# A written order for the middle stage of an attention and two-MLP kernel

## The chip, the cores and the metric

The kernel runs on one core of a Trainium2 chip. The metric is the device time of one execution in microseconds (us). A core has five engines with a queue each, and every queue is worked in order: PE (TensorE, matmuls; its weight loads are shown as PEld), DVE (VectorE), ACT (ScalarE), POOL (GpSimd) and SP (SyncE, which here issues nearly all DMAs). An instruction waits at the head of its queue until what it needs is done; what stands behind it waits too.

## The reference, cut to what matters

Linear attention over 8 batches, 8 heads, 576 positions and 64 channels, then two MLPs over 4608 tokens of width 512 with a hidden width of 2048, all in float32:

```python
q_s = exp(q - max(q, -1));  q_s /= sum(q_s, -1) + 1e-9
k_s = exp(k - max(k, 2));   k_s /= sum(k_s, 2) + 1e-9        # over the positions
kv = einsum('bhsd,bhse->bhde', k_s, v);  x = einsum('bhsd,bhde->bhse', q_s, kv)
h = x @ w_in;   x = (h * clip(h + 3, 0, 6) / 6) @ w_out       # first MLP
h = x @ w2_in;  out = (h * sigmoid(h)) @ w2_out               # second MLP
```

## The kernel before, in words

The 4608 tokens are nine blocks of 512. A block has four attention units, one for each pair of heads; unit u belongs to block u // 4, so there are 36 units. Float32 matmuls of the MLPs are made of three passes over operands that were split into a high and a low part (high x high, high x low, low x high), each 128x512; a split costs one copy on ACT (high) and one subtraction on DVE (low).

The program has three stages, and no barrier stands between them:

- `first_block()` (L852) computes units 0 to 7 and part of 8, splits the first MLP's weights, and runs the first MLP on block 0. `spin` (L873) adds matmuls without use to keep PE occupied at the start.
- `middle()` (L1017) computes the other units, runs the first MLP on blocks 1 to 6, splits and sums the weights for the second MLP and writes them to DRAM (`Parts`, `Resident`, `Split`), and prepares the first operands of the next stage (`first_operands`, L1265). Its main step (j, f) is `mm1` (L552, twelve 128x512 matmuls into a PSUM bank "h", in four chunks c), the gate of four jobs (`Gate`, L564: relu on ACT, times_h on DVE, upper on ACT, lower on DVE), and `mm2` (L621, twelve matmuls into y0 to y3: eight that need the gate's upper part alone, four that need the lower part). A unit's small PE jobs lie between these: `k_turn`, `k_spread`, `kv_mm`, `q_turn`, `x_mm`.
- `second_mlp()` (L1335) runs the rest by events in order of a clock of PE slots. Its first PE work is the product P1 with operand B11 (high and low), then P6 with T2, then the last `mm2` of the middle's steps (L1671), then P5 (T1), P2 (B21), P7 (T3), P3 (B22).

What sets the order in the first two stages is a planner, `Plan`. `add` (L748) notes a job: its engine, an assumed duration, a key, the jobs that it needs, and the buffers that it takes and gives back. `once` (L753) then plays the jobs through in Python while the program is built: whenever an engine is free, the ready job with the lowest key starts, if its buffers are free. The order in which jobs started is the order in which the instructions are written, and so that of each queue. `plan.run(0, 300e3)` (L1187) does this once for `middle`, with keys from the tables `LATE`, `WORK` and `FETCH`. Waits between engines come from data and buffers, whatever the order.

Buffers that matter here: "t2k" (five 128x512 temporaries), "sp" (three), "h" and "a" (two PSUM banks each), and the 128x128 tiles `kvt` of which there are `KVS` = 5, one for each unit's kv, used in turn. `k_max` (L360) puts its half-way maximum m2 into a t2k buffer. `kv_mm(u)` waits for `x_mm(u - 1)` in the planner, since its kv takes the place of an older one that `x_mm(u - 1)` reads last.

The operands of P1 to P7 come from four blocks of the first MLP's output (B12, B22, B11, B21, loaded by SP) by four sums on POOL (t3, t1, t2, t4, L1239) and seven splits: high parts on ACT (L1300), low parts on DVE (L1310). t2 is in place over t3's result and needs the split T3 done and t1; t4 is in place over t2's result and needs the split T2 done; T4 needs t4. B11 needs only that t2 and t1 have read it. In the order before, T1, T2, B11, T4, B21 and B22 follow each other over the last 55 us of the stage, and the B22 split is the only one that is left when the last `mm2` of the stage runs.

Of the kernel before, what the change touches and what calls it, by code (L numbers as in the profile page):

```python
# [28 lines left out]
def efficient_attention_then_two_mlps(  # L29
# [20 lines left out]
    KCH = S // P  # L50
    TAIL = S - KCH * P
    NU = B * NP
    KVS = NP + 1
    NCL = NB - 2
    FAR = 4
    LAG = (2, 3)
# [15 lines left out]
    ident = const.tile([P, P], F32, name="ident")  # L72
    minus = att.tile([P, DM], F32R, tag="sp", bufs=3, name="minus")[:, 0:P]
    peaks = const.tile([P, P], F32, name="peaks")
    kvt = [const.tile([P, P], F32, name=f"kv{i}") for i in range(KVS)]
    vbufs = const.tile([P, 2, KCH + 1, 2, D + 1], F32, name="vbuf")
    small = const.tile([P, 8], F32, name="small")
# [280 lines left out]


    def k_max(u):  # L360
        t = kbuf[u]
        m1 = peaks.rearrange("p (h d) -> p h d", h=2)
        m2 = tmp.tile([P, 8, D], F32, tag="t2k", name="m2")[:, 0:4]
        m2 = m2.rearrange("p (h a) d -> p h a d", h=2)
        nc.vector.tensor_tensor(out=m2, in0=t[:, :, 0:2, :], in1=t[:, :, 2:4, :], op=ALU.max)
        nc.vector.tensor_tensor(out=m1, in0=m2[:, :, 0, :], in1=m2[:, :, 1, :], op=ALU.max)
        nc.vector.tensor_tensor(out=m1, in0=m1, in1=t[:, :, KCH, :], op=ALU.max)
        live["m1", u] = m1
# [370 lines left out]
    class Plan:  # L739
# [277 lines left out]
    def middle():  # L1017
# [12 lines left out]
        def unit(u):  # L1030
            j, pr = divmod(u, NP)
            key = lambda r: begin[u] + r + 0.3
            old, has_k = u == NP * 2, u < NU
            if u > NP * 2 + 2:
                n_q[u] = dma(0.8, key(-3.4), lambda: load_q(u), 256, [qsub[u - 2]])
            if has_k and u > NP * 2 + 1:
                n_k[u] = dma(0.7, key(-3.5), lambda: load_k(u), 320, [ksub.get(u - 2)])
                n_v[u] = dma(1.0, key(-2.5), lambda: load_v(u), 320, [kvmm[u - 2]])
            kx = qn = None
            if not old:  # L1040
                qm = add("DVE", 0.7, key(0), lambda: q_max(u), [n_q.get(u)])
                qs = add("POOL", 1.1, key(1), lambda: q_sub(u, nc.gpsimd), [qm], ["qe"], [], True)
                qsub[u] = qs
                qx = add("ACT", 0.65, key(2), lambda: q_exp(u), [qs])
                qa = add("DVE", 0.7, key(2), lambda: q_sum(u), [qx])
                qa = add("POOL", 0.3, key(2), lambda: q_eps(u, nc.gpsimd), [qa])
                qa = add("DVE", 0.22, key(2), lambda: q_recip(u), [qa])
                qn = add("POOL", 1.1, key(2), lambda: q_norm(u, nc.gpsimd), [qa], [], [], True)
            else:
                qsub[u] = None  # L1050
            if has_k and not old:
                km = add(
                    "DVE", 1.1, key(0), lambda: k_max(u), [n_k.get(u)], ["m1", "t2k"], ["t2k"], True
                )
                kt = add("PE", 0.12, key(1), lambda: k_turn(u, a_pool), [km], ["a", "mx"], ["m1"])
                kd = add("DVE", 0.3, key(1), lambda: k_peak(u), [kt], [], ["a"])
                ks = add("PE", 0.12, key(2), lambda: k_spread(u, a_pool), [kd], ["a", "ke"], ["mx"])
                kx = ksub[u] = add("DVE", 0.85, key(2), lambda: k_sub(u), [ks], [], ["a"])
            if u < DIRECT:
                qt_ = add("PE", 0.65, key(3), lambda: q_turn(u), [qn], ["a"], ["qe"])  # L1060
                ql = add("ACT", 0.62, key(3), lambda: q_copy(u), [qt_], ["qT"], ["a"])
            else:
                qb = add("DVE", 0.72, key(3), lambda: q_blocks(u), [qn], ["t2k"], ["qe"])
                z0 = dma(0.35, key(3), lambda: q_store(u), 256, [qb], [], ["t2k"])
                ql = dma(1.4, key(4), lambda: q_load(u), 256, [z0], ["qT", "z"])
            if has_k:
                kx = add("ACT", 0.78, key(3), lambda: k_exp(u), [kx])
                mm = kvmm[u] = add(
                    "PE", 0.48, key(4), lambda: kv_mm(u, a_pool),
                    [kx, n_v.get(u), xmm.get(u - 1)], ["a"], ["ke"],  # L1070
                )
                va = add("DVE", 0.45, key(4), lambda: kv_sum(u), [mm])
                vlow[u] = add("ACT", 0.55, key(4), lambda: kv_scale(u), [va], [], ["a"])
            xm = xmm[u] = add(
                "PE", 1.0, key(6), lambda: x_mm(u), [ql, vlow.get(u), vlow.get(u - NP)], ["a"],
                ["qT"] if u < DIRECT else ["qT", "z"],
            )
            first = ["x"] if pr == 0 and j < NCL else []
            if j < FAR:
                xu = add(  # L1080
                    "ACT", 0.62, key(6), lambda: x_upper(u), [xm, xready.get((j, 0))], first
                )
                xready[j, pr] = add("DVE", 0.69, key(6), lambda: x_lower(u), [xu], [], ["a"])
                return
            xc = add("ACT", 0.62, key(6), lambda: x_upper(u), [xm], ["t2k"], ["a"])
            xs_ = dma(0.35, key(6), lambda: x_store(u), 256, [xc], [], ["t2k"])
            if j < NCL:
                at = j * NF - 14 + 2 * pr + FETCH[(j - FAR) * NP + pr]
                ld = dma(
                    0.35, at, lambda: load_x(j, pr), 256, [xs_, xready.get((j, 0))], ["t2k"] + first  # L1090
                )
                hi = add("ACT", 0.64, at + 1.5, lambda: x_high(j, pr), [ld])
                xready[j, pr] = add("DVE", 0.72, at + 1.5, lambda: x_low(j, pr), [hi], [], ["t2k"], True)
# [49 lines left out]
        for n, s in list(enumerate(steps))[NF - 1 : NCL * NF]:  # L1143
            ph, j, f = s
            g3 = g2 = None
            if n >= NF:
                m = None
                for c in range(NC):
                    m = add(
                        "PE", 0.69, n - 0.5, lambda s=s, c=c: mm1(s, [c]), [xready.get((j, c)), m],  # L1150
                        ["h"] if c == 0 else [],
                        (["x"] if f == NF - 1 and c == NC - 1 else [])
                        + (["wi"] if j == NCL - 1 and c == NC - 1 else []),
                    )
                free[n] = m
                g = Gate(s)
                g0 = add("ACT", 0.62, n - 0.45, g.relu, [m], ["r"])
                g1 = add("DVE", 0.7, n - 0.45, g.times_h, [g0], [], ["r"])
                g2 = add("ACT", 0.62, n - 0.45, g.upper, [g1], ["g"])
                g3 = add("DVE", 0.7, n - 0.45, g.lower, [g2], [], ["h"])  # L1160
                plan.held |= {g0, g1, g2, g3}
# [22 lines left out]
            else:  # L1184
                pair_at[at] = add(eng, us, base + key, fn, deps, take, [], port)

        for fn in plan.run(0, 300e3):  # L1187
            fn()

    pair_at = {}  # L1190
# [74 lines left out]
    def first_operands():  # L1265
# [11 lines left out]
        def load(name):  # L1277
            def do():
                operand(name, 1)
                x_steps(1)[name.lower()]()  # L1280
            return do
# [4 lines left out]
            ("r1", "SP", 0.35, 1.5, get(1), 512, ("r0",), ["wi"], False),  # L1286
        ]
        for n, name in enumerate(("B22", "B11", "B21")):
            jobs.append((name.lower(), "SP", 0.35, 2.5 + n, load(name), 512, ("r1",), ["wi"], False))

        def total(name, key, deps):
            jobs.append((name, "POOL", 2.1, key, lambda: x_steps(1)[name](), 0, deps, [], True))
# [455 lines left out]
```

## Time and profile before

| | us |
|---|---|
| median of three runs (1572.47 to 1573.20) | 1572.76 |
| the profiled execution | 1573.41 |
| its span, first to last instruction | 1571.70 |
| PE busy in the span | 1557.0 (99%) |
| DVE busy | 1115.9 (71%) |
| ACT busy | 761.0 (48%) |
| POOL busy | 489.2 (31%) |

The profile is that of one execution. A matmul's record lasts longer than its place in the row of matmuls: 128x512 matmuls start 0.227 us apart while each record lasts 0.39 us, so PE looks busy across any gap under some 0.17 us, and the start times tell more than the busy share. The same holds to a lesser degree on DVE and ACT. Middle's first PE instruction starts at 136.69 us and the second MLP's first at 715.90 us.

### The profile page before, as it was taken

To read this page: it belongs to the slowest core of one execution; us is meant where nothing else is said; L and a number is where in the kernel's file an instruction comes from. 1 tells how busy PE (TensorE), PEld (TensorE's weight loads), DVE (VectorE), ACT (ScalarE), POOL (GpSimd) and SP (SyncE) were. 2 spreads that over 40 slices of the span, in tenths; PEclk is the share of its full clock that TensorE was granted. 3 is DMA by queue.
4 is the path that set the end of the run, shared out by engine and by line. 5 is a ranking of instruction groups with operands and counts; after the bars stand their busy time and mean duration, and the time that the engine had idled before them with its cause. 6 is when DMAs were issued, how large, how long until landed. Compare 5 with 4: busy or idle time off the path is not lost.

```text
span 1571.7 us, 22243 instructions
## 1 busy us (share of the span) xinstructions
PE 1557.0 (99%) x7403; PEld 1272.4 (81%) x7403; DVE 1115.9 (71%) x1791; ACT 761.0 (48%) x1358; POOL 489.2 (31%) x446
## 2 busy tenths in 40 slices
PE   7999999999999999999999999999999999999999
PEld 4787878888888888888888888888888888888887
DVE  7989577776777776555689569856976797677732
ACT  6887345554555544443365236533643464345422
POOL 4334224433434335421232242234223422440000
PEclk9999999999999999999999999999999999999999
DMA  9915976776786855746566786765668875879850
GB/s 280 335 44 176 334 227 209 238 231 203 226 257 212 264 193 189 234 152 208 189 223 217 209 233 219 260 206 198 228 213 213 224 247 194 227 224 372 260 129 27
DMA packets 346226, 342.81 MB, mean 218 GB/s; under 512 B 126464, under 2 KB 252160, under 8 KB 346112
## 3 DMA queue, kind: packets, MB, share of 16 engines
q1 hardware_dynamic: 344496, 340.70, 68.3%
q8 instruction: 59, 0.97, 0.3%
q10 hardware_dynamic: 1616, 0.69, 0.2%
q14 instruction: 55, 0.45, 0.1%
HBM read 247.20 MB, written 94.11 MB: 217 GB/s over the span
## 4 chain that ended last, share of the span: by engine, by line
PE 95%; DVE 2%; ACT 1%; DMA 1%; POOL 1%; issue 0%; SPq 0%; DVEq 0%; ACTq 0%; POOLq 0%
PE pb L1366 24%; PE pb L1525 24%; PE h L559 21%; PE y L634 19%; PE y L636 3%; PE pa L513 2%; PE pa L412 1%; DVE fa L140 0%; PE pa L384 0%; DMA ahead<-in_q_dram 0%; DMA qraw<-in_q_dram 0%; DMA wi_early<-in_moe_w_in_dram 0%; PE pa L476 0%; PE busy L875 0%; PE pa L372 0%
## 5 line engine op out<-in xcount | busy, mean ns | idle before, releaser
L559 PE MATMUL h<-x,wi 128*128 128x512 f32 x1536 | 381.8, 396 | 2.0 <-POOL wi L165 0.9
L1366 PE MATMUL pb<-xo,ring 128*128 128x512 f32 x1680 | 383.0, 389 | 0.0
L1525 PE MATMUL pb<-gsp,ring 128*128 128x512 f32 x1680 | 382.4, 389 | 0.0
L1366 PEld LDWEIGHTS pb<-xo,ring 128*128 128x128 f32 x1680 | 315.3, 188 | 65.9 <-issue 0.5
L1525 PEld LDWEIGHTS pb<-gsp,ring 128*128 128x128 f32 x1680 | 315.3, 188 | 65.5
L559 PEld LDWEIGHTS h<-x,wi 128*128 128x128 f32 x1536 | 283.2, 188 | 65.2 <-POOL wi L165 1.9
L634 PE MATMUL y<-g,wo 128*128 128x512 f32 x1344 | 323.6, 390 | 0.0
L634 PEld LDWEIGHTS y<-g,wo 128*128 128x128 f32 x1344 | 251.3, 188 | 52.7
L1353 DVE TENSOR_TENSOR gsp<-g,gsp 128x512 fp32r<-128x512 f32 x240 | 184.4, 788 | 25.0 <-ACT gsp L1471 24.2
L1471 ACT CAST gsp<-g 128x512 fp32r<-128x512 f32 x240 | 143.6, 622 | 105.4 <-PE pb L1525 89.1
L599 DVE SCALAR_TENSOR_TENSOR h<-r,h 128x512 f32<-128x512 f32 x112 | 77.7, 693 | 108.4 <-ACT r L572 108.2
L572 ACT ACTIVATE r<-h 128x512 f32<-128x512 f32 x112 | 66.9, 597 | 175.1 <-PE h L559 173.2
L1353 POOL TENSOR_TENSOR xst<-xst 128x512 f32<-128x512 f32 x32 | 70.8, 2212 | 168.6 <-DVE xo L1353 84.5
L1353 DVE TENSOR_TENSOR g<-r,pb 128x512 f32<-128x512 f32 x96 | 65.7, 684 | 54.6 <-ACT r L1380 54.1
L1380 ACT ACTIVATE r<-pb 128x512 f32<-128x512 f32 x96 | 57.1, 595 | 97.2 <-DVE pb L1353 72.8
L1353 POOL TENSOR_TENSOR g<-g 128x512 f32<-128x512 f32 x40 | 53.5, 1337 | 148.6 <-DVE g L1353 123.4
L1353 POOL TENSOR_TENSOR s<-U,s 128x512 f32<-128x512 f32 x32 | 42.6, 1330 | 173.3 <-DVE U L1353 173.3
L590 ACT CAST g<-h 128x512 fp32r<-128x512 f32 x112 | 65.5, 585 | 48.8 <-DVE h L599 40.6
L593 DVE TENSOR_TENSOR g<-h,g 128x512 fp32r<-128x512 f32 x97 | 66.8, 689 | 28.6 <-ACT g L590 26.5
L1353 DVE TENSOR_TENSOR U<-pb,s 128x512 f32<-128x512 f32 x80 | 55.0, 688 | 17.0 <-PE pb L1366 12.5
L195 POOL TENSOR_TENSOR fa<-fa 128x256 f32<-128x256 f32 x64 | 49.9, 780 | 40.7 <-DVE sp L227 32.2
L1380 ACT ACTIVATE r<-s 128x512 f32<-128x512 f32 x32 | 20.2, 632 | 87.3 <-POOL s L1353 70.3
(160 smaller groups left out, 1751.4 us busy)
## 6 DMA issues: line engine op xcount, KB each, us to landing
ring<-ws SPq DMA_DIRECT2D x280, 512.0 KB, 3.9
ws<-sp SPq DMA_DIRECT2D x128, 256.0 KB, 3.2
wi_early<-in_moe_w_in_dram SPq DMA_DIRECT2D x16, 512.0 KB, 8.5
wo_early<-in_moe_w_out_dram SPq DMA_DIRECT2D x16, 512.0 KB, 9.2
wi_raw<-in_moe_w_in_dram SPq DMA_DIRECT2D x16, 512.0 KB, 4.7
ws<-w_sum SPq DMA_DIRECT2D x32, 256.0 KB, 3.1
ws<-fa SPq DMA_DIRECT2D x32, 256.0 KB, 2.8
wo_raw<-in_moe_w_out_dram SPq DMA_DIRECT2D x16, 512.0 KB, 4.4
```

Source lines behind the costliest of these rows:

```text
L195: lambda to=to, x=x, y=y, op=op: nc.gpsimd.tensor_tensor(out=at[to], in0=at[x], in1=at[y], op=op)
L559: nc.tensor.matmul(h, w[:, a, c, :], x[:, e, c, :], start=(c == 0 and n == 0), stop=(c == NC - 1 and n == 2),)
L572: nc.scalar.activation(self.r, self.h, AF.Relu, bias=3.0)
L590: nc.scalar.copy(self.g[:, 0], self.r)
L593: nc.vector.tensor_tensor(out=self.g[:, 1], in0=self.r, in1=f32(self.g[:, 0]), op=ALU.subtract)
L599: nc.vector.scalar_tensor_tensor(out=self.h, in0=self.r, scalar=6.0, in1=self.h, op0=ALU.min, op1=ALU.mult)
L634: nc.tensor.matmul(y[c], w[:, a, cs], g[:, e, :], start=st, stop=sp)
L1353: (eng or nc.vector).tensor_tensor(out=out, in0=a, in1=b, op=how)
L1366: nc.tensor.matmul(to, ws_[:, a], e[:, c], start=p in ("P1", "P6", "P5") and c == 0 and m == 0, stop=c == 1 and m == 2, skip_group_check=True,
L1380: nc.scalar.activation(r, d[b, n, key], AF.Sigmoid)
L1471: nc.scalar.copy(t[0], source(p, i))
L1525: nc.tensor.matmul(d[b, p][m], w[:, a, m * P : (m + 1) * P], t[e], start=new and i == 0 and k == 0, stop=i == NPR - 1 and k == 2, skip_gro ...
```

## The change

`middle` no longer asks the planner. A string of 2374 two-character numbers (base 64, `DIGITS`) lists its jobs, numbered in the order in which `add` was called, and `plan.listed` writes them in that order. The first block is still ordered by the planner's `once`, with the same jobs.

Three other edits change instructions: `k_max` writes m2 into a tile of its own (`halved`) in place of a t2k buffer; `KVS` is 6 in place of 5, so that one more `kvt` tile is cleared at the start and a kv stays one unit longer. The edits to the arguments of `add` in `middle` and `first_operands` change what a planner would see; the jobs and their numbers stay the same.

```diff
+MIDDLE = (
+    "K8090VK-"
...
+    "aZaQaRaaabK5ayaiajb4b5azb0b1a-a_Cwb2b3AVaw"
+)
+def listed(text):
+    at = [DIGITS.index(x) for x in text]
+    return [64 * a + b for a, b in zip(at[::2], at[1::2])]
...
-    KVS = NP + 1
+    KVS = NP + 2
...
+    halved = const.tile([P, 2 * P], F32, name="halved")
...
-        m2 = tmp.tile([P, 8, D], F32, tag="t2k", name="m2")[:, 0:4]
-        m2 = m2.rearrange("p (h a) d -> p h a d", h=2)
+        m2 = halved.rearrange("p (h j d) -> p h j d", h=2, j=2)
...
+        def listed(self, order):
+            jobs = self.jobs
             return [jobs[i][3][0] if jobs[i][0] in ("SP", "AQ") else jobs[i][3] for i in order]
...
-                    "DVE", 1.1, key(0), lambda: k_max(u), [n_k.get(u)], ["m1", "t2k"], ["t2k"], True
+                    "DVE", 1.1, key(0), lambda: k_max(u), [n_k.get(u)], ["m1"]
...
-                    [kx, n_v.get(u), xmm.get(u - 1)], ["a"], ["ke"],
+                    [kx, n_v.get(u)], ["a"], ["ke"],
...
-                m = None
+                m = free.get(n - 1)
...
-        for fn in plan.run(0, 300e3):
+        for fn in plan.listed(listed(MIDDLE)):
             fn()
...
-            jobs.append((name.lower(), "SP", 0.35, 2.5 + n, load(name), 512, ("r1",), ["wi"], False))
+            jobs.append((name.lower(), "SP", 0.35, 2.5 + n, load(name), 512, ("r1", "b12"), ["wi"], False))
```

The list's last jobs, by queue (jobs 2350 to 2373 are the operands; "sp" is a weight split of `Split`, step 14 is `mm1` and gate of block 6, f = 14):

| queue | last jobs in the written order |
|---|---|
| PE | mm1 step 14 (three chunks), mm1 step 15, mm2 step 12 (last four matmuls), x_mm 35, mm2 step 13, mm2 step 14 |
| ACT | relu 14, three times sp high, upper 14, relu 15, T2 high, x_upper 35, upper 15, B22 high, T4 high, B11 high, B21 high |
| DVE | three times sp low, times_h 14, sp low, times_h 15, lower 14, T2 low, lower 15, B22 low, T4 low, B11 low, B21 low, T1 low |
| POOL | weight sum, t1, three weight sums, t2, t4 |
| SP | four stores of sp, x_store 34, a store of sp, a resident weight's store, x_store 35 |

## Rows read from the trace of the kernel before

**Rows 1.** The profile's page, busy time of each engine over the span.
```profile
PE 1557.0 (99%) x7403; PEld 1272.4 (81%) x7403; DVE 1115.9 (71%) x1791; ACT 761.0 (48%) x1358; POOL 489.2 (31%) x446
```
**Rows 2.** Windows by stage: stretch, length, busy PE, PEld, DVE, ACT, POOL, clock, DMA.
```profile
0.00:136.69 136.69, 126.22 (x666) 95.17 (x667) 118.33 (x230) 106.89 (x199) 46.57 (x57) 0.99 0.61 196
136.69:715.90 579.21, 578.54 (x2980) 471.91 (x2978) 399.94 (x695) 282.38 (x511) 222.40 (x246) 1.00 0.70 225
```
**Rows 3.** Longest of PE's two waits in the middle stage: total, times, longest.
```profile
PE pa L412 <- ACT ke L403: 0.4, 1, 0.4
```
**Rows 4.** Timeline of PE around these waits: start, length, instruction, idle before.
```profile
149.05 0.27 PE L384 MATMUL pa<-ident,small 128*128 128x128 f32 x1
149.56 3.04 PE L559 MATMUL h<-x,wi 128*128 128x512 f32 x12 [0.23 <-DVE g L593]
152.43 1.03 PE L513 MATMUL pa<-qt,kv 128*128 128x128 f32 x4
154.64 1.67 PE L634 MATMUL y<-g,wo 128*128 128x512 f32 x6
```
**Rows 5.** The same pairs of jobs without a wait, PE timeline.
```profile
198.77 1.03 PE L513 MATMUL pa<-qt,kv 128*128 128x128 f32 x4
200.47 2.10 PE L634 MATMUL y<-g,wo 128*128 128x512 f32 x8
...
315.53 0.27 PE L384 MATMUL pa<-ident,small 128*128 128x128 f32 x1
315.55 2.98 PE L559 MATMUL h<-x,wi 128*128 128x512 f32 x12
318.37 2.88 PE L634 MATMUL y<-g,wo 128*128 128x512 f32 x12
```
**Rows 6.** PE timeline, mm2 to mm2: round kv_mm and mm1, then with k_spread behind kv_mm.
```profile
289.03 2.88 PE L634 MATMUL y<-g,wo 128*128 128x512 f32 x12
295.45 2.88 PE L634 MATMUL y<-g,wo 128*128 128x512 f32 x12
...
323.96 2.88 PE L634 MATMUL y<-g,wo 128*128 128x512 f32 x12
330.44 2.88 PE L634 MATMUL y<-g,wo 128*128 128x512 f32 x12
```
**Rows 7.** PE timeline from the end of the middle's last mm1 into the second MLP.
```profile
712.71 2.89 PE L634 MATMUL y<-g,wo 128*128 128x512 f32 x12
715.44 1.02 PE L513 MATMUL pa<-qt,kv 128*128 128x512 f32 x2
719.05 2.88 PE L634 MATMUL y<-g,wo 128*128 128x512 f32 x12
```
**Rows 8.** The same stretch on ACT, DVE and POOL: gate jobs, operand splits, a sum.
```profile
712.97 0.60 ACT L572 ACTIVATE r<-h 128x512 f32<-128x512 f32 x1 [3.42 <-PE h L559]
713.47 1.04 ACT L1300 CAST xo<-xo 128x1024 fp32r<-128x1024 f32 x1
714.41 0.58 ACT L590 CAST g<-h 128x512 fp32r<-128x512 f32 x1
...
715.02 0.69 DVE L593 TENSOR_TENSOR g<-h,g 128x512 fp32r<-128x512 f32 x1 [0.73 <-ACT g L590]
715.63 1.22 DVE L1310 TENSOR_TENSOR xo<-xo 128x1024 fp32r<-128x1024 f32 x1
...
686.19 2.39 POOL L1239 TENSOR_TENSOR spare<-xo,spare 128x1024 f32<-128x1024 f32 x1 [14.67 <-DVE xo L1310]
```
**Rows 9.** Windows around the only fall of the clock (columns as in rows 2).
```profile
17.00:19.00 2.00, 0.46 (x3) 0.28 (x3) 1.93 (x8) 0.24 (x1) 0.53 (x1) 1.00 0.98 340
19.00:22.50 3.50, 3.50 (x12) 2.71 (x12) 2.44 (x6) 2.69 (x5) 2.31 (x4) 0.51 1.03 380
```
**Rows 10.** Timeline of DVE: the same instruction alone, and beside sums on POOL.
```profile
129.90 0.68 DVE L140 CUSTOM_DVE_ANT_0 fa<-fa,fr 128x1024 uint16<-128x1024 uint16 x1
...
144.99 1.77 DVE L140 CUSTOM_DVE_ANT_0 fa<-fa,fr 128x1024 uint16<-128x1024 uint16 x1
```

More of the change, by code (lines that the diff above doesn't have):

```diff
@@ L21 @@
 LOWEST = -3.4028234e38
+DIGITS = "0123456789ABCDEFGHIJKLMNOPQRSTUVWXYZabcdefghijklmnopqrstuvwxyz-_"
+MIDDLE = (
+    "K8090VK-"
+    "L8K_L4L2L6L70GL9LAL5LBLILC0001LJDYLKLDLLL0020H0I03L1HU0AAWAXLELGLFLH0B0C0DLMLSLTLU0J0XLN0tAYAZHW0ELO"
+    "LPAeAa04LVEC0F0L0MAyLcLdLeLf050K06L3AbLWLQLR0O0Y1G0PAc0e0Z0a0u0bAd07LX0c0wLgLhAxAgLY0dLZ08Li0jLmLnLo"
+    "LpLq0fLjGq0gLw0h0Q0N0RLaLbLk0iAf0kAh0x1fAzA-A_LlB0LxLr0S1HB1AiLsLyLzB2B3B40y0z11120-0W0_101617L-"
+    "1J0m1K22LtB8LuM4M5L_1L0l131M1NM01OM10TAj1PM6LvB5B6B70n1IAkM7M8Al1iM2M9MA1V1W0o0pMB0vMEBH1j1k1l1mMFMG"
+    "MHMI0U2RM3AmAnAoApB9MOBBMC1nMJMKML0qMDBABCBDBEBF1oMP1u1vMQMR25MSAtAuMYBbBGBdMTMUMZMa14151gBIMbMV2UMM"
+    "MNMWMcMd1QBKJS1RMeMXBeBJ0rMi0sMj19MfBfBgBh1ABiBj26271B1CBLIo1pMkMlMsAqAr1SMm18MnMoMpAs28BMMgMhMqMtMu"
+    "MvMw292A2B2H2qDaMx2t1T2V2W1UMyMzMrBkAvAwBl1q1rBmBNBON02XBo2Y2ZCE2aBQBR1YBnN1N2N3NAN4N5M-"
+    "M_N6N7BpNB2gBqBS1ZNC1a1b2INDNENF23NGNH1D1ENKCF1hBPN8CH1F1s1t2h1xCI1XBrBsN9NLNM2CBTBXBYBUNNNUCJCK1y1z"
+    "NONPNQNVNWBVNXNY2D2ECLBZNI1-"
+    "1c1dNRNZ1eNJ2FNmNnNoNa3GNbNpBtBuBvNS24NTNwNcNdNqNrNsNtBWCMBxBy1wCN3JNgNxNyNz2G2KO42uN-N_BzB-B_COCPO0"
+    "O1O5O6NiC01_O7O8O92LOENh2TBw2v2SNkC1Cv20OFNe2M2NOGCQCR2bOHOIOJC2C4C5NuNv2wOAOBNlO22x2yO3OCOKC6C72c3i"
+    "CBOO2dOPOQOLCxC3CyNfC8CS2zCz332eGs34ODCTOROYOZOaObOSOT2JOUC9OV3KCCOcOdCA3LC-C_CVCUD0D13M3NOMONOW2f3O"
+    "3POe2sOi2jOj3lOkOlOmD2Of2OCD2P3VCWCX3W48CbOnOsOtOuOvCYCZOwOxIqOXOg2Q3mOh213n3oOyOz4aD3CcCeFY2k2l4BCd"
+    "CfP0OoOpD42r3p3q2iP1P2P3OqNjPAPBCgOrO-O_P4P5P63rCa3x4C4DP7ChCiD52mPCPDD6P8D7D92-"
+    "2_PKDFPL3031PMD8PN4E2nPEPFPGCjCkClDA32PHDB3HDGP9PIDCDD2o352pCm3yPJ3jDE36373Q3RCnCoCpPUPVPWPOCqPPPQDH"
+    "PXPRDZDbDcDdPSDIPe3sPYPZPfPa4F3SPgPhPb38Po4GPpDePT4HPiDJPqPrDK3IDmGCPjPkDLPc393ADMDN4NPl4O50PsPt3B3C"
+    "DfDgPd3T3U3YCrDhPuPvPyPzP-PmCsPn4dP_49Q0PwQ1DnDoDpDqDrDiCtDOQ6DPDQ3Z3a3t3uQ24IQ73bQ8Q93kDRDVDW3XQAKm"
+    "Q3PxDXQB3v4J4KQCQ4Q53wQEQOEDDjDSDk4bDT4e4fQDDl533-"
+    "QFQG4g5S4hQKDU3_QP4L4MQMEFEG4iQQQRQY4jQNQL4kDvQSQTQUQZ404p4ADsQVQaEHQbQIQJ3c3dQHQcQdQeQfQWQX41DwQiDx"
+    "QjQkDyDzD-"
+    "4lQlQs54Qm55564mQtQuEIQgQhQnDtEJQo5u4QQpEtQvQw3z42435758R0R1595V3e515ADuQx4R4q5F4SQyEKEL4P5W44R2R3EM"
+    "4n4o5XQqEvEw6K5YQr5G3DD_5B4cExR4R55Z5xQz5a5bQ-Q_R6R7RAE0E1R8RBRCE2RD5hENEO5y5z5-"
+    "E34TEPR93ERERFRGRHE4E552Ey5TRKRLE6RME9EAE7EQ5_60613F5i4sE8RNRURO3f5CRVEBEzE-RW4t4uRX5DRI6N4vRP5UGAER"
+    "ESRYRZRJRQRaET5E5IRRRSRTRcReRb67E_F06OEUEVEWEXRf3g3h68EZ4U4VRg5c6P6Q6mRhRiRjRkRlRoRpRqRrRs6R4W5J5KEa"
+    "5d6S6TRyRzR-"
+    "5v6pEYRd5LEbEcEdRmRnF1F25eRtEeRuEfRvEgEiR_Ej4r6ZS0S1454647S6S74XF3RwS2S84Y4ZS3F4F5F6RxS9EkElF7SGF85w"
+    "EmEsEnF9SHEhFXSASBSCEo5fSDS4S5SE6q6rSIFDSJ5g6L5kSQFA6a7C6s6t6u6vFBFCFZSKSLFEFFSFFGSMFHSNFa4wIA624x6_"
+    "70SREpSSSTSaSUFISVEq5H63645lSOSWSXSP6M5m7FFJFKSbScSd6UFL5nSkFk6VSeSfSgSlSmSn65SoSYErSh6W7e7G7H84FMFN"
+    "FOT0FPFb4yFT5MFcFdFeFfFgSZSi666AFUSjT1T2FQT36BSp5jFRFSSq7I7JSsFl5NFmT4FnFhSr6CFiFoT5FpGBGDTA5O6XFV6Y"
+    "T6FjStSwSyS-"
+    "T7TBSxTCTD7K7LTESzGESuTFTGFt6n7R5oTHTKTLTMTN7hSvT86DTOT9TIS_7STPTQTUTR69GFGG7iTJ5pTVTWTXTeTfFq7DFrGH"
+    "Fs87GIGJ6c5qFuTSFwFvFxTYTZTaFyFzF-G0TgTh4z6EGK4-"
+    "G1TT6dFWF_GOGL6F6G4_5PTbGMToG2TiTjTk7jTpTqTcTrTlGPTs6wTtG3G4G5G7G8Td6x6yTuGNTyTzT-T_Tv7MTmTn7N7E6e6f"
+    "U0Gr6z6-CuGR727OG66oGtGu7kGQGSU6U1GvG9U7U86HU9GT7lKoUAGUTwGVGwU2U373GxGyGzTxU4GX6bG-UB7PUC7m7n7tUD7Q"
+    "8TUGUHUI7UUJUK8889U5UEG_7uULUQUFGYGa74GW75UMUR8sH0H1GZGbGc8A8BUSUNGdGeGgGhUT5QUUCG8WGfUOUP8C7fUV8D8J"
+    "GiGjUWUX6IGnUaUb8X8Y9FUcUdUk5RUeGo8ZHVHXH2GkUfUgUh6g718K6hUYUZGp8a8b6JGl7V7W7X8c7oK69I8iUlUmUnUo85Uu"
+    "UvUwUpUq7pHYH3H57qUrHZHaHbGmH4H6H7H8UxUyUi6iUjUs76HcHd868j7rUzH977U-"
+    "U_V2V3V4V5V6HB7s7w8vUtV0V17gHCHDVCHAV7VDVE8E8F5rHEV8HFHGHeV9HH8wHI8xHKHL8UHMHNVFVGVH7x7THJVMVNVOVP7y"
+    "VAI9HO8y8GVIVJVB8HVQ8z8-"
+    "78HfHgVKVeHh7zIBIC9eVRVSVTEEHRHSHTVL7YVU8I8MVV8_5s5tHiVfVg8d8eVcVdID8fIEIFIGVWVXHPHQVhViVj95Vk8tVlIH"
+    "VaVbVY8NVoVpVqVrVs9J9KVtVyVzV-VuV_96VmHjHkVvVn9LW0W1W69sIIW7W8W9VwHlVxW2W3W49MHm8VI8HnHrWG90WAWB7v7Z"
+    "7aWCWDIJVZIK9N9OW5HsHt9UHoHpHuHvWHWIWJWQWRWKWLWM8g8h9fWNWEWFWO8OWP91HqHwHx9VHy92WS8PWTILH-WUWVHzWaWb"
+    "WcIMWd8uH_I0I1WWEuWX7-"
+    "BcI5WeWfI6INWkWlI7I2I3IPWm8lWnWgIV7_WYWZWiIOIQWhWu809tIRWo9uWp9v9w8mIpIrI4IsISWvWq9394WrIT9G8LWjWwWx"
+    "9x6jWyWsX2IWWzW-8QWtX0W_X19PX3AIIYIXIZIU8RItIuIaX4IvX5XCXDIw98IxIy9y6k6lIbIc9z9-"
+    "X6XEXFX7X89QX98SJ09gA4XAXB7b81XMXG9RXH8nXIXJ7c9h9iIz99XNXOXPXWXXIeIfI-XYXQXR9_IgIhIdIl7dXKImXLXSXT9j"
+    "9k9l9A9mI_9n8283XZXaXgXhXiXjXbXcXd8o9BJ1JTJVJWJXJYJ3XUXVXe8kXqXrXsXkXl9HXfXmXoJZJaInXnJ2IiIjIkJ4J5AJ"
+    "K7K9XtXuA5XvXwA6JbX-X_XxA7A88pY0A9Y1YG79Y2Y39S9TXp7A7BJcAAABXyXzYHYIYJY48qY6Y58rY7JdJeYQYRYS97YKYLYM"
+    "YAYNJfYCACKAJUYTYUYaKBKCKDYb9CY8YcYdKEYVYBJgAKYWYXADYEJ6akJ7Y9BaYkYlALJhAMANJ8KFKGYmJiYnYoYp9XYeYfYO"
+    "YPYYYgYhJjJkYD9Y9Z9aYFJlJmJnYuYvYwYZAO9WJ99bAPKHKIKJJoYxYyYzKnA0YiKpYqJAKqYrYjYs9D9EYtY-JBJCJDJEY_am"
+    "JFKrKsKtJGJIJpZ2Z3Z0JHZ49cZ59dZCZDZEZFZ6Z7Z8KuJJJKZ1Z9ZMZGJLZHZIJPZNZOZPA1ZJJMZAAQKvZWZQZXARZBZRalan"
+    "JqZYJNJOJQKwJRZKZLJsJrJt9oJuZSZTZZZaA2A3ZbKKZgKxZhZiaqKyKzZjZkJvZcZdZUZV9pJwJyZqJxZeAEZrKLKMJzZsZtKN"
+    "aoKOJ-ZlZmZfZoKPZuZvZnJ_ZwKQZ-Z_a0a1ZxKTKRKUa2KVKWa3KXa8a9KYKS9q9rZpZyapZza4KZKaa5aAaBKcaCaDK0AFaEaI"
+    "ASaraFaJaKaLaSKda6AGa7aGKeasaMaNavaTaUKbKfataOaPaVaWK1K2KjKkacadaeafKlKgKhaXKiaHK3ATaYK4AHagahauaxAU"
+    "aZaQaRaaabK5ayaiajb4b5azb0b1a-a_Cwb2b3AVaw"
+)
@@ L360, in k_max @@
     def k_max(u):
-        t = kbuf[u]
-        m1 = peaks.rearrange("p (h d) -> p h d", h=2)
-        m2 = tmp.tile([P, 8, D], F32, tag="t2k", name="m2")[:, 0:4]
-        m2 = m2.rearrange("p (h a) d -> p h a d", h=2)
+        t, m1 = kbuf[u], peaks.rearrange("p (h d) -> p h d", h=2)
+        m2 = halved.rearrange("p (h j d) -> p h j d", h=2, j=2)
         nc.vector.tensor_tensor(out=m2, in0=t[:, :, 0:2, :], in1=t[:, :, 2:4, :], op=ALU.max)
@@ L820, in run @@
                     span, order, keys = end, got, tried
+            return self.listed(order)
+        def listed(self, order):
+            jobs = self.jobs
             return [jobs[i][3][0] if jobs[i][0] in ("SP", "AQ") else jobs[i][3] for i in order]
@@ L1069, in unit @@
                     "PE", 0.48, key(4), lambda: kv_mm(u, a_pool),
-                    [kx, n_v.get(u), xmm.get(u - 1)], ["a"], ["ke"],
+                    [kx, n_v.get(u)], ["a"], ["ke"],
                 )
-                va = add("DVE", 0.45, key(4), lambda: kv_sum(u), [mm])
-                vlow[u] = add("ACT", 0.55, key(4), lambda: kv_scale(u), [va], [], ["a"])
+                va = add("DVE", 0.45, key(4), lambda: kv_sum(u), [mm, vlow.get(u - 2)])
+                vlow[u] = add("ACT", 0.55, key(4), lambda: kv_scale(u), [va, xmm.get(u - KVS + NP)], [], ["a"])
             xm = xmm[u] = add(
```

## Prediction

> **What bounds the kernel now.** I read the page first, then the windows by stage, the waits of PE and PE's timeline. The page says that PE is busy for 1557.0 us, 99% of the span, at nearly the full clock [rows 1]; DVE, ACT and POOL are far from full. By stage, middle is 579.21 us long and PE is idle for 0.67 us of it, while the first block leaves over 10 us [rows 2]. So what the change may win in middle is small from the start: the view of waits shows only two for PE there, 0.4 us before a kv_mm [rows 3] and the 0.23 us that its timeline shows too [rows 4]. Since a matmul's record outlasts its slot, the true loss is read from start times: k_spread to the next mm1 takes 0.51 us at 149.05 where 0.02 us is normal, and x_mm with kv_mm takes 2.21 us at 152.43 where the same pair takes 1.70 us elsewhere [rows 4, 5]. That is 0.49 + 0.51 = 1.0 us, both in the first 20 us of the stage. From there on 128x512 matmuls follow each other at 0.227 us. A measurement of this kernel can tell about 0.2% (3.1 us) from no change, so a perfect middle would not show as faster.
>
> **The change, part by part.**
>
> *Stalls that go.* At best 1.0 us. What replaces them at the entry of the stage is a list that starts with eight matmuls of mm2 whose operand is long there, so I take -1.0, with 0 as the other bound.
>
> *Interruptions of the matmul stream.* The work on PE is the same, but its small jobs stand otherwise: in the order before they form 73 runs between mm1 and mm2 (x_mm and kv_mm together eleven times, kv_mm and k_spread six times), in the list 91 runs, mostly of one job. What one more interruption costs is read from mm2 to mm2: with kv_mm between, 6.42 us; with kv_mm and k_spread, 6.48 [rows 6]; k_spread alone adds 318.37 - 315.53 - 12 x 0.227 = 0.12 [rows 5]. So standing together saves 0.12 - 0.06 = 0.06. Eighteen more runs cost 0 to 1.1 us; some of the joint runs save less than this one, so I take +0.6.
>
> *Waits inside the stage.* A gate's chain from the end of mm1 to mm2 is 0.26 until relu starts, then 0.60 + 0.69 + 0.58 [rows 7, 8], 2.1 us and some 0.2 for hand-overs. In the order before, at least one mm2 and one mm1 (5.4 us) stand between. In the list this cover has a larger median, but it falls below 3.5 us in a handful of the 95 steps, the least being step (5, 9) with one mm1 and a small job, 2.8 us. So the list has room almost everywhere and 0.5 us where it is tightest: +0.2, bounds 0 and 1.
>
> *The entry of the second MLP.* Here the list differs most, and I follow it with zero at the end of the last mm1 (step 15; 712.71 in the rows). PE then has four matmuls of mm2 (0.91), x_mm 35 (719.05 - 715.44 - 2.72 = 0.89 [rows 7]) and two whole mm2 (5.44): it reaches P1 at 7.24, and P1's second matmul, which reads the low part of B11, is due at 7.47. What must happen first:
> - relu 14 starts at -2.72 + 0.26 and ends at -1.86. On DVE two subtractions that need the sp highs behind it on ACT stand before times_h 14, which so runs from about -0.2 to 0.5. Upper 14 waits for it, relu 15 stands behind upper 14 on ACT: 1.05.
> - T2 high (1.04 long, 0.94 until the next [rows 8]) stands behind relu 15: 1.55 to 2.6. T2 low on DVE, behind times_h 15 and lower 14 at 0.61 each: 2.85 to 4.05.
> - POOL's t4 overwrites what T2 reads, 2.39: to 6.5. T4 high stands before B11 high on ACT: 6.55, then 7.5 to 8.55. T4 low stands before B11 low on DVE: B11 low runs from 8.8 to 10.0.
>
> B11 itself could be split long before; it is late because it stands behind T4 in two queues, and T4 behind POOL. PE waits 10.0 - 7.47 = 2.5 us. One sp high before upper 14 also waits for an sp buffer, which comes back when a store lands; that may add up to 0.7. I take +2.8, bounds 2.3 and 3.3. In the order before, all this is done and only B22 is left [rows 8]. After P1 nothing else is late: P6 needs T2 (4.05), P5 follows P6 and an mm2 and finds T1 (about 13) in time. Nothing wins it back, as PE has no slack later.
>
> *The other edits.* The sixth kvt tile is one more small clear on DVE before its first load has landed, and k_max does the same three operations on another tile: 0 in both, between -0.5 and 0.5, since fewer temporaries are shared in the busy first block. On SP the weights' stores are spread instead of standing in front; x_store 35 still stands before the ring fetches of the second MLP, whose first reader, P7, comes more than 10 us later, now behind the wait too: 0.
>
> **Sum.** -1.0 + 0.6 + 0.2 + 2.8 + 0 = +2.6 us. The profiled execution, 1573.41 (span 1571.70 and 1.71 around it), would become 1576.0; it stands 0.65 above the median, so for the median I say 1572.76 + 2.6 = 1575.4. This case's own range is 1574.2 to 1576.6: 0.17%, no change within 0.2% by a little.
>
> **The rivals.**
>
> *The clock falls at the entry (slower).* The wait for B11 leaves PE with one matmul in about 2.7 us. The clock fell once in this trace, to half (0.51 over 3.5 us, 1.2 in place of 2.4 GHz), after 2 us in which PE was busy for 0.46 [rows 9]. That is about as thin as the wait would be; against it, the stream before and after is dense here, and it was not there. If it decides so, half of 3.5 us is lost on top: +1.75, 1577.1, slower. The Trainium skill, page "TensorE: Matmul & The Clock Gate", section "Why this matters for your kernels", warns of idle gaps between bursts of matmuls because the clock then goes back to half; by that rule the time is this rival's, and the trace agrees with its one fall.
>
> *The wait at the entry is hidden.* If ACT and DVE run ahead more than I read, or times_h 14 is not held, B11 is there in time; the rest of the sum is -0.2, so about 1572.5. For it: each link is only some 0.1 to 1 us from another order of events. Against it: T2 high cannot pass relu 15, and from there on the chain has no choice.
>
> *Collisions in the list's tight places (slower).* A DVE instruction that takes 0.68 us alone takes 1.77 beside POOL's sums [rows 10]. If some four of these hit the few steps whose cover is only 0.5 to 1 us above the chain, they cost up to 3 us more: 1578.4. It decides from the point where DVE is late by more than that cover.
>
> *The first block gains.* With m2 out of the shared temporaries, its 10 us of idle PE [rows 2] could shrink by several us: about 1569. But its order is the same and its waits are for chains of DVE and ACT.
>
> **How the numbers follow.** Forecast 0.45, clock 0.23, hidden wait 0.18, collisions 0.09, first block 0.05. Some four fifths of the forecast's chance and all of the hidden wait's lie within 0.2%: 0.35 + 0.18 = 0.53. Slower: 0.10 + 0.23 + 0.09 = 0.42. Faster: 0.05. The range takes in the forecast, the hidden wait, the clock and the nearer half of the collisions: 1572.0 to 1578.4.
>
> **What would show it.** Right: in the timeline of PE the first matmul of L1366 is followed by a gap of 2 to 3 us, the view of waits names DVE or ACT with xo for it, POOL's last L1239 ends shortly before, and middle from its first PE instruction to this point is as long as before within 1 us. The clock's row at this place decides the first rival. Wrong: no gap before or in P1, or waits of PE over 2 us elsewhere in middle.

## The result and the profile after

The changed kernel takes 1582.63 us (median), the kernel before beside it 1572.74: the ratio is 1.0059 with an interval of 1.0041 to 1.0076. It is 0.6% slower, the interval excludes 1, and the time lies above the range. Three of its four runs took 1582.6 us; the fourth took 1580.06 us and left no trace. The profiled execution took 1582.64 us, its span is 1580.9.

Three views of the kernel after answer to the page and the windows of before [rows 1, 2]. First the page's line of busy times, then the windows by stage (columns as in rows 2), with two short stretches at the entry of the second MLP behind them:

```profile
PE 1560.8 (99%) x7403; PEld 1272.1 (80%) x7403; DVE 1117.2 (71%) x1792; ACT 758.2 (48%) x1358; POOL 492.2 (31%) x446
```
```profile
0.00:136.27 136.27, 124.80 (x667) 93.98 (x668) 118.48 (x231) 106.81 (x199) 46.68 (x57) 1.00 0.63 199
136.27:721.51 585.24, 581.02 (x2980) 470.80 (x2978) 400.16 (x692) 279.22 (x512) 224.06 (x246) 1.00 0.71 224
721.51:1580.90 859.39, 854.94 (x3759) 707.32 (x3759) 598.54 (x871) 372.20 (x648) 221.48 (x144) 1.00 0.69 215
719.11:721.90 2.79, 0.99 (x4) 0.36 (x2) 2.76 (x3) 2.44 (x3) 0.32 (x1) 1.00 0.97 328
721.90:728.70 6.80, 5.85 (x15) 4.50 (x15) 3.86 (x4) 1.09 (x2) 0.00 (x0) 0.50 0.44 170
```

PE's busy share is again 99%, as it was before: this line tells nothing. The stages tell more. The stage `middle` is 6.03 us longer than the 579.21 of [rows 2], the second MLP 859.39 - (1571.70 - 715.90) = 3.59 us longer. The last line shows most of why the second MLP is longer: for 6.8 us behind its first matmul the granted clock is 0.50, the lower of the two levels (1.2 GHz in place of 2.4).

The place itself, in PE's timeline (start, length, instruction, idle before), which answers to [rows 7]:

```profile
713.21 1.02 PE L578 MATMUL pa<-qt,kv 128*128 128x512 f32 x2
713.67 6.04 PE L699 MATMUL y<-g,wo 128*128 128x512 f32 x24
721.51 0.50 PE L1435 MATMUL pb<-xo,ring 128*128 128x512 f32 x1 [1.80 <-ACT xo L1369]
722.96 5.06 PE L1435 MATMUL pb<-xo,ring 128*128 128x512 f32 x11 [0.95 <-DVE xo L1379]
727.82 3.35 PE L699 MATMUL y<-g,wo 128*128 128x512 f32 x12
731.00 2.20 PE L1435 MATMUL pb<-xo,ring 128*128 128x512 f32 x9
```

Read it by start times. The last of the 24 matmuls of mm2 starts at 719.32, so P1 could start at 719.55; it starts at 721.51 (1.96 lost), and its second matmul 1.45 later in place of 0.227 (1.22 lost). That is a wait of 3.19 us. From 722.96 to 731.00 lie 23 matmuls, 5.21 us at 0.227 each; they take 8.04. That is 2.83 us for the clock.

PE's waits in the middle and at its end (total, times, longest), where [rows 3] had 0.4 us and one other wait of 0.2:

```profile
PE pb L1435 <- ACT xo L1369: 1.8, 1, 1.8
PE pa L437 <- DVE peaks L432: 1.6, 3, 1.1
PE pb L1435 <- DVE xo L1379: 0.9, 1, 0.9
PE y L699 <- ACT o L719: 0.5, 1, 0.5
PE pa L449 <- ACT kv L494: 0.3, 1, 0.3
```

The first and the third are the entry. The second stands in no term of the prediction's sum: k_turn (L437) waits for the last operation of k_max (L432). Measured from matmul to matmul, as in the prediction, six places inside the stage cost more than the same jobs cost elsewhere: 0.50 at 196 us, 1.14 at 302, 0.17 at 330, 0.84 at 343 to 345, 0.43 at 424, 0.49 at 473, together 3.57 us.

The whole account, in starts of PE instructions: the first mm of the stage comes 0.47 earlier (136.22 for 136.69); from there to where P1 could start are 583.33 us for 579.61 (716.31 in the kernel before, P1's second matmul less one slot), +3.72; the entry costs 3.19 + 2.83 = 6.02; all that follows is equal. -0.47 + 3.72 + 6.02 = +9.3, and the spans differ by 9.2. The 0.47 can't be put down to the change: in ten profiled runs with this same first block (this one and the nine below) the first mm of the stage starts anywhere between 135.75 and 136.60 us.

### The profile page after: what moved, and what is told of

It reads as the page before. It is cut to its first block, busy times and chain, and to the rows that moved or that the text cites. A ratio compares the mean times of both kernels' runs of the same rounds, so it can differ in the third digit from the quotient of the medians.

```text
span 1580.9 us, 22184 instructions
## 1 busy us (share of the span) xinstructions
PE 1560.8 (99%) x7403; PEld 1272.1 (80%) x7403; DVE 1117.2 (71%) x1792; ACT 758.2 (48%) x1358; POOL 492.2 (31%) x446
## 4 chain that ended last, share of the span: by engine, by line
PE 93%; DVE 3%; DMA 1%; ACT 1%; SPq 1%; issue 1%; POOL 0%; DVEq 0%; ACTq 0%; POOLq 0%
PE pb L1435 24%; PE pb L1594 24%; PE h L624 20%; PE y L699 17%; PE y L701 3%; PE pa L578 2%; PE pa L477 1%; DMA wo_early<-in_moe_w_out_dram 0%; DMA kbuf<-in_k_dram 0%; DVE fa L207 0%; DVE h L664 0%; DVE fa L211 0%; DVE halved L430 0%; SPq L173 0%; PE pa L437 0%
## 5 line engine op out<-in xcount | busy, mean ns | idle before, releaser
L699 PE MATMUL y<-g,wo 128*128 128x512 f32 x1344 | 330.3, 394 | 0.5 <-ACT o L719 0.5
L533 POOL TENSOR_TENSOR qe<-qe,qs 128x512 f32<-128x512 f32 x36 | 40.1, 1114 | 71.7 <-DVE qs L529 45.2
```

The source lines that it names most:

```text
L699: nc.tensor.matmul(y[c], w[:, a, cs], g[:, e, :], start=st, stop=sp)
```

## Experiments

Every kernel is the changed one with the edit shown; job numbers are those of the list. `moves` stands for these lines in `middle`:

```diff
-        for fn in plan.listed(listed(MIDDLE)):
+        order = listed(MIDDLE)
+        for job, place in MOVES:
+            order.remove(job)
+            order.insert(order.index(place) + 1, job)
+        for fn in plan.listed(order):
```

The theory: three losses that add, namely B11 behind T4 at the entry, the fall of the clock which that wait sets off, and turns of k's maxima that stand right behind maxima stretched beside POOL. The rivals: the clock falls for a reason of its own; DVE and ACT are behind as a whole in this order, so that mending one place only moves the wait; the other edits cost something. The kernel before, run beside them, took 1572.96, 1572.78 and 1572.85 us in the three groups of runs.

### B11 ahead of T4

```diff
+        MOVES = (2366, 2364), (2367, 2366), (2362, 2367)   # B11 high, B11 low, T1 low behind T2 low
```


> B11's split goes back ahead of T4's (and T1's lower half up with it). If the 3.6 us of PE idle at the entry of the second MLP come from B11's place behind T4, both waits go and PE's first matmul of the second MLP starts 0.1 us after mm2(14); if the fall of the clock from 721.9 to 728.7 us is set off by that idle time, it goes too: about 6.4 us less, 1576.2. If the clock falls by itself at this change of stage (it fell at 19 us in the kernel before without such a wait), 3.6 us less, 1579.0. If ACT and DVE are late here anyway, whatever the order of the splits, the wait stays and the time too.

Measured: 1576.64 us (ratio to before 1.0024, 1.0015 to 1.0034), 5.99 less than the change. PE's timeline:

```profile
713.24 6.04 PE L699 MATMUL y<-g,wo 128*128 128x512 f32 x24
719.11 2.88 PE L1439 MATMUL pb<-xo,ring 128*128 128x512 f32 x12
721.83 2.88 PE L699 MATMUL y<-g,wo 128*128 128x512 f32 x12
```

No idle time is shown and the 12 matmuls up to the next line take 2.72 us. Wait and clock are gone together, 3.19 + 2.83 = 6.02. The 3.6 us of the expectation were 0.43 too much: that much of the time before P1 belongs to the x product in front of the 24 matmuls, which take 5.87 us here (713.24 to 719.11) and 24 x 0.227 = 5.45 without it. Three operand jobs in other places of two queues are worth 6 us; ACT and DVE were not late as a whole here.

### The wait stays, PE is kept busy in it

```diff
+            if (b, n, p) == (0, 0, "P1"):
+                for _ in range(16):
+                    nc.tensor.matmul(
+                        to, w[:, 0, 0:P], op["T3"][0][:, 0],
+                        start=True, stop=True, skip_group_check=True,
+                    )
```


> The order of the change stays, and so does the wait for B11; PE runs 16 matmuls of 128x512 (16 x 0.227 = 3.6 us), whose result is thrown away, in the wait. If PE's idle time sets off the fall of the clock, 0.5 in the windows after 721.9 us becomes 1.0 and 2.8 us are won: about 1579.8. If the clock falls for another reason, the time stays at 1582.6. If the fill is longer than the wait, up to 0.5 us are lost on top of either.

Measured: 1580.17 us, 2.46 less. The fill ends 0.44 later than the wait would, so the clock was worth 2.46 + 0.44 = 2.9:

```profile
719.34 3.79 PE L1434 MATMUL pb<-xo,ring 128*128 128x512 f32 x16
722.97 2.88 PE L1441 MATMUL pb<-xo,ring 128*128 128x512 f32 x12
```

The order of the jobs is the same, P1 starts as late as before, and the clock stays at 1.00 in every window from 716 to 729 us. So it fell because PE stood idle. The rival "by itself" is out.

### Turns behind the stretched maxima, one or two matmul jobs later

```diff
+        MOVES = (91, 1441), (219, 1631), (415, 1839), (424, 1913), (1708, 230)
+        # k_turn 12, 17, 24; kv_sum 24 (on DVE); mm1 of step (3, 2), first chunk
```


> Inside the stage alone: the turn of k's maxima of units 12, 17 and 24 stands one or two matmul jobs later on PE, a sum of kv (unit 24's) ahead of unit 26's maxima on DVE, and one job of mm1 between the products of unit 17's x and the mm2 that waits for y. If the 3.6 us of new stalls are those turns, standing right behind maxima that a POOL sum stretches, these five places (0.50, 1.14, 0.43, 0.49 and 0.50 us) give back 2.5 to 3.0 us: about 1579.9, with the entry as it is. If another operation is late just behind each of them (DVE and ACT as a whole are behind in this order), the stalls only move and the time stays within 0.5 us of 1582.6.

Measured: 1579.75 us, 2.9 less. In the profiled run P1 could start 2.49 us earlier than in the change, 0.18 of them won before the stage and 2.31 in it. (Its span is 3.5 shorter, since its clock fell for 3.4 us in place of 6.8.) At unit 17 the kernel after and this one read as follows, first after:

```profile
301.48 0.91 DVE L430 TENSOR_TENSOR halved<-kbuf 128x256 f32<-128x256 f32 x1
302.43 0.70 DVE L431 TENSOR_TENSOR peaks<-halved 128x128 f32<-128x128 f32 x1
303.17 0.76 DVE L432 TENSOR_TENSOR peaks<-peaks,kbuf 128x128 f32<-128x128 f32 x1
...
302.19 1.59 POOL L262 TENSOR_TENSOR w_sum<-w_sum 128x256 f32<-128x256 f32 x2
...
302.17 0.80 PE L477 MATMUL pa<-vbuf,ke 128*64 128x65 f32 x20
304.07 0.30 PE L437 MATMUL pa<-ident,peaks 128*128 128x128 f32 x1 [1.10 <-DVE peaks L432]
```
```profile
301.51 0.80 PE L477 MATMUL pa<-vbuf,ke 128*64 128x65 f32 x20
302.24 1.65 PE L624 MATMUL h<-x,wi 128*128 128x512 f32 x6
303.73 0.27 PE L437 MATMUL pa<-ident,peaks 128*128 128x128 f32 x1
303.76 1.40 PE L624 MATMUL h<-x,wi 128*128 128x512 f32 x5
```

The maxima are as slow as ever, but six matmuls of mm1 now run meanwhile, and k_turn waits for nothing. Four of the five places mended so. The fifth, at 343 us, did not: I had taken its wait for y as its cause, and the move only changed which job waits, as PE's waits inside the stage show:

```profile
PE h L624 <- DVE g L658: 0.6, 1, 0.6
```

Now it is a job of mm1, for a gate's lower part. What is late there is again k_max, unit 20's (340.1 us in the kernel after, 2.5 us long), which stands on DVE ahead of a gate's product.

### The planner's order, all other edits kept

```diff
-        MIDDLE = ( the written order )
+        MIDDLE = ( the same jobs in the order of the kernel before )
```


> The middle's jobs in the order of the kernel before, given as a list; all other edits of the change stay (the buffer of its own for the halved maxima, the sixth kv tile, the first block). If the written order carries the whole loss, this gives the time of the kernel before less the 0.5 us by which the first block ends earlier: 1572.2. If the other edits cost something too, it stays above 1573. If they help, through the freer buffers, it goes below 1572.

Measured: 1572.63 us, ratio 1.0000 (0.9990 to 1.0009). So the list carries the whole loss; `halved`, the sixth kv tile and the first block are worth 0.3 us or nothing. Its two waits are the old ones [rows 3, 4]:

```profile
PE pa L469 <- ACT ke L460: 0.4, 1, 0.4
PE h L616 <- DVE g L650: 0.2, 1, 0.2
```

### Both places mended

```diff
+        MOVES = (2366, 2364), (2367, 2366), (2362, 2367),
+            (91, 1441), (219, 1631), (415, 1839), (424, 1913), (302, 1695)   # the last: k_max 20
```


> The moves of the first and the third experiment together, and unit 20's maxima on DVE behind the gate's product and lower half that they held up (0.78 us of PE wait). If the terms add, the entry's 6.0 us and the stage's 2.3 us, as those two runs showed them, and up to 0.8 us for unit 20 are won: 1582.6 - 6.0 - 2.3 - 0.8 = 1573.5, which leaves the 0.7 us of the more numerous runs of small jobs against the kernel before. If they are alternatives (a stage that ends earlier only waits longer at the entry), it stays near the 1576.6 of the first experiment.

Measured: 1573.46 us, ratio 1.0005 (0.9996 to 1.0014). The terms add, and eight moves among 2374 jobs take the loss back. The view of waits names none for PE between 136 and 730 us, and yet the time is no better than the planner's with its two waits. What is left I put down to the 91 interruptions in place of 73; that is by subtraction, and no run tests it alone. By start times P1 could begin at 716.10 here and at 715.42 in the planner's order, which still has its 1.0 us of waits, so 0.7 + 1.0 - 0.15 (the one at 330 us, left as it was): some 1.5 us.

### The planner's order with its two waits mended

```diff
+        MIDDLE as in the planner's order
+        MOVES = (1348, 1369), (1349, 1348), (24, 20)   # a copy of y and its store; k_exp 9
```


> The order of the kernel before with the change's other edits, and its two waits inside the stage mended by one move each: a copy of y on DVE goes behind the gate's operations at 146 us (0.50 us of PE wait), unit 9's exponentials on ACT go ahead of a gate's relu at 151.8 us (0.51 us). If a wait in front of PE is worth its length in this stage, 1.0 us less than the planner's order: 1571.6. If DVE and ACT only hand the delay on, 1572.6.

Measured: 1571.51 us, 1.1 less than the planner's order; ratio to before 0.9992 (0.9983 to 1.0001). A wait in front of PE is worth its length. But the profiled run, the slowest of its eleven, shows a new one at 539 us:

```profile
PE y L691 <- ACT o L711: 0.4, 1, 0.4
```

### POOL's sums narrowed

```diff
-                out=at[to], in0=at[x], in1=at[y], op=op
+                out=at[to][:, 0:32], in0=at[x][:, 0:32], in1=at[y][:, 0:32], op=op
```


> The change's order untouched; POOL's sums of weights run over 32 of 256 columns, so the rest of these sums is left out. If the stretch of the maxima (1.3, 0.7 and 0.8 us in place of 0.42, 0.29 and 0.29) comes from these sums beside them, the waits at 302, 343, 424 and 472 us go (1.1 + 0.7 + 0.4 + 0.5), those beside the queries' differences at 196 and 330 us stay, and the time falls by about 2.5 us, to 1580.1. If the maxima are late in DVE's queue whatever POOL does, the waits stay and so do the 1582.6 us. The entry is not touched by either.

The kernel leaves out 224 of the 256 columns of these sums. Measured: 1578.44 us, 4.2 less. P1 could start 2.9 us earlier, a little more than expected since the wait at 196 us went too, and the clock fell for one stretch only (the other 1.3, by subtraction; its five runs lie between 1575.89 and 1579.47, so this share is rough). The same unit 17, nothing moved:

```profile
301.24 0.91 DVE L430 TENSOR_TENSOR halved<-kbuf 128x256 f32<-128x256 f32 x1
302.19 0.29 DVE L431 TENSOR_TENSOR peaks<-halved 128x128 f32<-128x128 f32 x1
302.51 0.29 DVE L432 TENSOR_TENSOR peaks<-peaks,kbuf 128x128 f32<-128x128 f32 x1
...
302.95 0.30 PE L437 MATMUL pa<-ident,peaks 128*128 128x128 f32 x1 [0.22 <-DVE peaks L432]
```

Two of the three operations fall from 0.70 and 0.76 to 0.29 us, and k_turn comes 1.1 earlier, 0.24 of it because the three start earlier. The first operation stays at 0.91: it runs beside another kind of POOL operation (L339), which keeps its full width here. The whole stage says the same. Of the 69 operations of k_max in the trace of the change 18 are stretched, all beside a TENSOR_TENSOR of POOL, and of the other 51 one has such a neighbour; with the sums narrowed 6 are stretched, each beside a POOL operation of full width. The stretch is POOL's doing. The Trainium skill, page "SBUF — State Buffer", section "Who interferes with whom", says that a DVE instruction with two inputs in SBUF contends with a GpSimd instruction that reads SBUF, because they share a read interface; all three operations of k_max have two such inputs, and the trace agrees.

### B11 last, in the planner's order

```diff
+        MIDDLE as in the planner's order
+        MOVES = (2366, 2372), (2367, 2373)   # B11 high and low behind B22 high and low
```


> The order of the kernel before (with the other edits) and one thing of the written order alone: B11's split goes behind B22's, to the end of the stage. By the rows of the run in the planner's order ACT ends B22's upper half at 713.6 and a gate's at 714.1, so that B11's is there at 715.2, and DVE's lower half behind B22's at 717.2; PE's first matmul of the second MLP stands at 715.0, its second needs the lower half. If the place of B11 alone makes the wait, 1.9 us are lost behind the first matmul: 1574.5. If so short a wait also lets the clock fall, 1.4 or 2.8 us more: 1575.9 or 1577.3. If the wait in the change came from DVE and ACT being late as a whole, nothing is lost: 1572.6.

Measured: 1576.02 us, 3.4 more than the planner's order, near the middle value of the expectation. PE's timeline, and the windows behind the wait:

```profile
715.75 0.79 PE L1431 MATMUL pb<-xo,ring 128*128 128x512 f32 x1
718.84 4.37 PE L1431 MATMUL pb<-xo,ring 128*128 128x512 f32 x11 [2.29 <-DVE xo L1375]
```
```profile
719.00:722.50 3.50, 3.50 (x10) 2.73 (x11) 0.00 (x0) 0.59 (x1) 0.00 (x0) 0.57 0.98 284
722.50:726.00 3.50, 3.50 (x16) 2.85 (x15) 1.36 (x2) 0.00 (x0) 0.00 (x0) 0.94 1.04 388
```

One operand in the wrong place of two queues, and nothing else of the written order, gives the same picture: a wait of 2.4 us (the second matmul was due at 715.75 + 0.43 + 0.23), where 1.9 had been expected, then the clock at half for one stretch, 1.7 us more. (This profiled run stands near the upper end of its runs, so the two make more than the 3.4 us between the medians.)

### Two more moves

```diff
+        MOVES = those of the planner's order with two waits mended, and (2022, 2038), (669, 2345)
```


> The sixth experiment with two more moves: on ACT a copy of y goes ahead of the exponentials and the gate's copy that stood before it at 537 to 539 us (PE waited 0.54 and 0.11 us for it there, a wait that the sixth run shows anew), and on PE the last x product, whose bank the second MLP's P6 takes, stands one gate's mm2 earlier (the first 12 matmuls of the second MLP take 3.15 us up to the next line where they take 2.72 without a wait: 0.43 us). If both waits are worth their length, 1.1 us less than the sixth run: 1570.4, 0.15% below the kernel before. If the copy of y only comes to wait for a free buffer, or the x product for its queries, half of that or nothing: 1571.0 to 1571.5.

Measured: 1571.60 us, ratio 0.9992 (0.9983 to 1.0001): a miss, the same as with two moves. PE's timeline shows where each went:

```profile
538.68 5.70 PE L691 MATMUL y<-g,wo 128*128 128x512 f32 x24
...
711.34 3.32 PE L691 MATMUL y<-g,wo 128*128 128x512 f32 x12
714.50 2.88 PE L1431 MATMUL pb<-xo,ring 128*128 128x512 f32 x12
```

At 539 us the wait is gone (24 matmuls in 5.7 us), and this span is 0.6 us shorter than that of the kernel with two moves, whose profiled run was its slowest; the medians don't show it. The 0.43 us that I had put down to a wait for P6's bank were none: they moved with the x product, and the 12 matmuls behind it take 3.32 now wherever it stands. Each of these two kernels is 1.2 to 1.3 us below the kernel before, at the edge of what these runs can tell.

## Why the prediction was wrong, point by point

- **Stalls that go, -1.0:** right. The old two waits don't appear in the list, and mending them alone gave 1.1.
- **Interruptions, +0.6:** right in kind, too small. In the profiled pair it is 3.72 + 1.0 - 3.57 = 1.15 us; the kernels without waits in the two orders say some 1.5. I had priced one pattern that joins jobs and let the others go.
- **Waits inside the stage, +0.2, bounds 0 and 1:** this is the step that failed. It came to 3.6, and the prediction's own sign of being wrong, waits over 2 us elsewhere in middle, came true (2.4 in the view of waits). Of the 6.7 us between the forecast's +2.6 and the +9.3 of the profiled pair, 3.4 lie in this step and 2.8 in the clock, to which the sum gave nothing. I had followed one chain, from mm1 over the gate to mm2, through all 95 steps, and given no time to any other pair. Four of the six waits stand at another pair, k_max to k_turn, which the list puts next to each other. The other two stand at a copy of y behind a gate (343 us) and at a sum of kv (473 us), each behind maxima on DVE. Those at 473 us take their usual 1.06; what is stretched there is a weight split's subtraction ahead of them, 1.22 us, and 0.74 with POOL's sums narrowed. For the pair, from the end of the third maximum to the start of k_turn are less than 0.6 us for six of 23 units; in the kernel before the least is 1.3. And the price was in its trace. Three rows of it that I had not read, on DVE, with the turn that follows on PE:

```profile
515.26 1.27 DVE L365 TENSOR_TENSOR m<-kbuf 128x256 f32<-128x256 f32 x1
516.56 0.71 DVE L366 TENSOR_TENSOR peaks<-m 128x128 f32<-128x128 f32 x1
517.30 0.78 DVE L367 TENSOR_TENSOR peaks<-peaks,kbuf 128x128 f32<-128x128 f32 x1
...
526.75 0.27 PE L372 MATMUL pa<-ident,peaks 128*128 128x128 f32 x1
```

  The three take 2.8 us there and 1.07 where POOL rests, and nobody minds, because the turn comes 8.7 us later. Nine of the 23 units of the stage have stretched maxima in the kernel before, eight in the kernel after. The list did not make them slower; it took away the distance that hid them.
- **The entry, +2.8, bounds 2.3 to 3.3:** right, near the upper bound. It came to 3.19, by the chain as told: POOL's t4 runs from 717.03 to 719.43, T4 high and B11 high follow each other on ACT, T4 low and B11 low on DVE.

```profile
717.03 2.40 POOL L1308 TENSOR_TENSOR spare<-xo,spare 128x1024 f32<-128x1024 f32 x1 [9.45 <-DVE xo L1379]
...
719.46 1.04 ACT L1369 CAST xo<-spare 128x1024 fp32r<-128x1024 f32 x1 [0.90 <-POOL spare L1308]
720.42 1.99 ACT L1369 CAST xo<-xo 128x1024 fp32r<-128x1024 f32 x2
...
720.54 1.22 DVE L1379 TENSOR_TENSOR xo<-spare,xo 128x1024 fp32r<-128x1024 f32 x1
721.68 2.36 DVE L1379 TENSOR_TENSOR xo<-xo 128x1024 fp32r<-128x1024 f32 x2
```

- **The other edits, 0:** right: with the planner's order -0.1 to -0.3 against the two medians of the kernel before, within the noise.
- **The rivals** failed as a set. I had set them up as alternatives, each in place of the forecast, and given the chance of each to its own time alone. But the fall of the clock is a consequence of the entry's wait, and the collisions lie elsewhere in the stage; both came true on top of it. The clock's price for one stretch, 1.75, was right (the run with B11 last shows 1.7), but in the profiled run the fall lasted twice as long, 2.83. The page of the Trainium skill named in the prediction ("TensorE: Matmul & The Clock Gate", section "Why this matters for your kernels") advises against idle gaps of PE between bursts of matmuls, since the clock then goes back to half. The traces agree: it fell in each of the four kernels with an unfilled wait and in none of the others at this place. The collisions were the right mechanism at the wrong place. Had I added the three, 1572.76 + 2.6 + 1.75 + 3.0 = 1580.1; that the 3.0 lies near the 3.57 measured would have been luck, as it was priced for hits on gates.

## What to carry to other kernels

A new order of old jobs is judged by distances: for every pair of producer and consumer, how far apart were they, how far are they now, and how long is the producer at its worst in the trace, not at its usual. Producers that share something with another engine (here DVE operations with two SBUF inputs beside POOL's operations) need the distance of their worst case. And a wait in front of PE is to be priced with what it does to the clock: rivals that can happen at once are added before the range is drawn.

## What I had not expected

- Behind a wait of 2.4 us on PE, with matmuls at the full clock on both sides, the granted clock was at half for 3.4 us, and behind one of 3.19 for 6.8 us in the change and for 3.4 in the runs with later turns and with narrowed sums. So the clock cost between half and nine tenths of what the wait did (1.75 or 2.83 for 3.19, 1.7 for 2.4). What decides between the two lengths these runs don't show.
- Behind an x product of two 128x512 matmuls the next job's first matmul starts 0.03 us after the product's second one, by its record, and its own second 0.64 later in place of 0.227 (713.64, 713.67 and 714.31 in the change). These 0.4 us look like a wait of the next job; they move with the product when that is moved.
- The stretched maxima are not stretched evenly: 0.42 us becomes up to 1.29, 0.29 up to 1.06, and with POOL's sums of weights at an eighth of their width 6 of the stage's 18 stretched operations are left.
